# Attention scores in four half-height products, row sums in PSUM and head loads on one queue

## The chip, the cores and the metric

The kernel runs on one core of a Trainium2 chip. The engines that matter here are TensorE (PE in the profile), VectorE (DVE), ScalarE (ACT), GpSimd (POOL, which here only starts DMA transfers and clears a few tiles) and SyncE (SP, which only starts DMA transfers). Matmul results go to PSUM, which has eight banks of 512 fp32 values per partition. The metric is the device time of one execution in microseconds. Of the kernel before, three runs gave a median of 1306.28 us (1305.25 to 1308.36).

## The reference

Attention over 8 batches, 8 heads, 576 tokens and a head size of 64, in which every score more than tau below its row's maximum is dropped, is followed by a two-layer network on 4608 rows of 512 with a rational activation:

```python
scores = scale * np.matmul(q, k.transpose(0, 1, 3, 2))
thresh = np.max(scores, axis=-1, keepdims=True) - tau
scores = np.where(scores >= thresh, scores, -1000000000.0)
scores = scores - np.max(scores, axis=-1, keepdims=True)
attn = np.exp(scores)
attn = attn / (np.sum(attn, axis=-1, keepdims=True) + 1e-09)
x = np.matmul(attn, v)            # then heads side by side: 4608 x 512
h = x @ w_in                      # 512 x 2048
P = a[0] + a[1] * h + a[2] * h2 + a[3] * h3          # h2 = h*h, h3 = h2*h
Q = 1.0 + np.abs(b[0]) * np.abs(h) + np.abs(b[1]) * h2
out = (P / (Q + 1e-06)) @ w_out   # 2048 x 512
```

## The kernel before

**Units.** Attention is worked in units. A full unit is 128 query rows of a pair of heads of one batch (32 pairs, four full units each, 128 in all); a rest unit holds the last 64 query rows of both heads (32 in all). The pairs are visited twice or once each, in a fixed order of 160 units. A pair's queries lie in one tile QQ, head 0 on partitions 0 to 63 and head 1 on 64 to 127, its keys likewise in KK; there are two buffers of each.

**One full unit** goes through these steps.

- Scores (f_qk, lines 805 and 809). Two fp32 products over 64 partitions, one per head, give the first 512 keys; a third over 128 partitions, from key columns that are zero in the other head's half, gives the last 64 keys of both heads. The scores fill three banks of PSUM. The first 21 units alternate between banks 0 to 2 and banks 3 to 5; from then on every unit uses banks 0, 1 and 2, so a unit's products can start only when the unit before has been read. Head 0 has columns 0 to 575 of the three banks, head 1 columns 960 to 1535, so the middle bank, bank 1, holds the tail of head 0 and the head of head 1.
- Row maximum (line 815, DVE), threshold (822 on ACT or 824 on DVE).
- Per head a Prelu activation on ACT (830) that moves the scores from PSUM into an SBUF tile e. When both heads are through, the three banks are free.
- Per head an exponential on ACT (834), in place in e, whose row sum is written by a second record, ACTIVATION_READ_ACCUMULATOR, into a small SBUF tile st.
- The sum's reciprocal (839 on ACT or 841 on DVE, then 845 on DVE), the probabilities as a high and a low fp16 part (339 or 341, and 856), two DMA transposes from SP (866), and the product with the values (925).

**The network** is worked in chunks: first-layer products (1042), a move to SBUF on ACT (1051), a chain of about ten elementwise steps that alternates between DVE and ACT (1056 to 1092), and second-layer products (1101).

**What sets the order.** The program is straight-line code. A planner (class Plan) is given each operation with an engine, a duration, a key and the operations that it needs, and lists them by a simple timetable of its own; two tables, TURN and KIND, shift the keys. Every engine then executes its own list strictly in that order, and an instruction that waits holds up everything behind it on its engine. The planner knows the buffers and the banks of the scores, and reckons with the times at which they come free. The waits in the built program come from the layer below, which follows what each instruction reads and writes and adds semaphores; two engines that touch the same PSUM bank are put in program order by it. The planner has "DMA" for SP and "GD" for POOL among its engines. Loads of queries and keys of the first eight pairs go out from SP, later ones from POOL; the two visits' first key loads from ACT.

Of the kernel before, what the change touches and what calls it, by code (L numbers as in the profile page):

```python
# [16 lines left out]
AX = mybir.AxisListType  # L17

# [19 lines left out]
SINGLE = 21  # L38
# [12 lines left out]

FROM_ACT = 2
# [25 lines left out]
EARLY = {"ACT": 1.2900, "DVE": 3.3863}  # L78
EARLY_END = 714.5248
PRICE = {"ACT": 1.0645, "DVE": 2.1978}  # L80

TURN = [
# [21 lines left out]
KIND = [  # L104
# [8 lines left out]
LOADS_END = 120.0  # L113
# [22 lines left out]
class Plan:  # L136
# [20 lines left out]
    def op(self, eng, dur, key, fn, after=(), take=(), drop=()):  # L157
        engs = {eng: dur} if isinstance(eng, str) else eng
        o = Op(engs, key, fn, [x for x in after if x is not None], list(take), list(drop))
        o.turn, o.kind = self.turn, self.kinds.setdefault(fn.__code__, len(self.kinds))  # L160
# [26 lines left out]
    def order(self):  # L187
# [19 lines left out]
        left = len(self.ops)  # L207
        while left:
# [38 lines left out]
            if e == "DMA" and o.drop and t < LOADS_END:  # L247

                o.dur = 2.0 * o.dur + 1.0
# [22 lines left out]
            for d in o.then:  # L272
                d.wait -= 1
                for x in d.engs:
                    d.ready[x] = max(d.ready[x], end + (self.OWN[e] if x == e else self.TO.get((e, x), self.LAT[e])))
# [14 lines left out]
def masked_attention_rational_ffn(  # L290
# [86 lines left out]
    QW = S + REM  # L377
    QQs = [const.tile([P, QW], F32, name=f"QQ{i}") for i in range(NQ)]
    KKs = [const.tile([P, QW + REM], F32, name=f"KK{i}") for i in range(NQ)]
    for t in QQs:  # L380
        nc.gpsimd.memset(t[:, NT * P:], 0.0)
    for t in KKs:
        nc.gpsimd.memset(t[0:D, S:QW], 0.0)
        nc.gpsimd.memset(t[D:P, 0:REM], 0.0)
# [899 lines left out]
```

## Time and profile before

| | |
|---|---|
| median of three runs | 1306.28 us |
| the profiled execution, its own time | 1312.41 us |
| its span | 1310.6 us |
| TensorE clock granted | 0.986 |
| busy: PE, DVE, ACT, POOL | 1253.8, 1217.9, 1114.4, 243.4 us |

The profile is of one execution. Busy time of PE is from modelled ends of pipelined matmuls, so that one matmul overlaps the next; busy times of DVE and ACT are those of their instructions. A name such as "banks" is the PSUM tile, "L834" is a line of the kernel before. In the kernel after, the same lines stand some lines lower: the scores at 807, the exponential at 840, the reciprocal's first step at 845 and 847, the transposes at 872, the two layers at 1048 and 1107.

### The profile page before, as it was taken

The numbers are of one execution on the slowest core, as the hardware profiler recorded it, in microseconds if no ns is written. First come the engines' busy times: TensorE is split into PE (matmuls) and PEld (weight loads), VectorE is DVE, ScalarE is ACT, GpSimd is POOL, SyncE is SP. The second block draws the span as 40 slices with busy tenths as digits, with TensorE's granted clock in tenths as the row PEclk, the third lists the DMA queues.
The fourth block names the chain that finished last, engine by engine and source line by source line (L and its number), as shares of the span: only waits on it lengthen the run. The fifth ranks groups of instructions, "written<-read, shape, count | busy, mean of one in ns | idle before, by whom it ended". The sixth has DMA issues, their size and how long they took to land. (4 is left out here: it accounts for less than half of the span.)

```text
span 1310.6 us, 25351 instructions
## 1 busy us (share of the span) xinstructions
PE 1253.8 (96%) x9430; PEld 931.8 (71%) x9430; DVE 1217.9 (93%) x1913; ACT 1114.4 (85%) x2182; POOL 243.4 (19%) x462
## 2 busy tenths in 40 slices
PE   8898989999999999998999979999999999999998
PEld 6576677777677777776777657766677777778886
DVE  5899999999999999988999979999999999999777
ACT  5898998999999999997999878978998798885564
POOL 1101100023213220323112231223213221110000
PEclk8998999999999999999999989999999999999999
DMA  7433454476656565677554875676756654563000
GB/s 206 132 116 125 142 128 87 105 160 119 124 116 134 124 131 107 117 143 129 95 103 96 115 132 100 122 126 119 137 106 115 132 131 75 109 111 55 17 17 17
DMA packets 340587, 146.66 MB, mean 112 GB/s; under 512 B 316208, under 2 KB 323184, under 8 KB 340464
## 3 DMA queue, kind: packets, MB, share of 16 engines
q1 hardware_dynamic: 316400, 86.49, 37.4%
q0 software_dynamic: 22784, 57.31, 16.4%
q8 instruction: 74, 1.21, 0.4%
q10 hardware_dynamic: 1280, 1.25, 0.4%
q14 instruction: 49, 0.40, 0.1%
HBM read 60.30 MB, written 9.44 MB: 53 GB/s over the span
## 5 line engine op out<-in xcount | busy, mean ns | idle before, releaser
L1101 PE MATMUL banks<-wp,g 128*128 128x512 f32 x1728 | 442.1, 404 | 1.6 <-DVE g L1092 1.2
L1042 PEld LDWEIGHTS <-wi 128*128 128x128 f16 x3456 | 333.6, 98 | 67.1 <-issue 29.0
L1042 PE MATMUL banks<-x,wi 128*128 128x256 f16 x3072 | 360.8, 274 | 10.0 <-ACT t L1051 9.3
L1101 PEld LDWEIGHTS banks<-wp,g 128*128 128x128 f32 x1728 | 315.9, 189 | 75.3 <-DVE g L1092 4.0
L834 ACT ACTIVATE e<-e,cf 128x576 f32<-128x576 f32 x288 | 222.1, 778 | 0.2
L856 DVE SCALAR_TENSOR_TENSOR e<-e,st,hi 128x576 f16<-128x576 f32 x252 | 204.6, 812 | 7.5 <-ACT hi L339 6.4
L339 ACT ACTIVATE hi<-e,st 128x576 f16<-128x576 f32 x223 | 169.6, 769 | 46.8 <-DVE st L845 30.8
L830 ACT ACTIVATE e<-banks,st 128x576 f32<-128x576 f32 x288 | 206.3, 737 | 3.0 <-DMA pT<-e 0.8
L815 DVE TENSOR_REDUCE st<-banks 128x2 f32<-128x1152 f32 x128 | 172.4, 1347 | 16.2 <-PE banks L809 15.8
L805 PE MATMUL banks<-KK,QQ 64*128 64x512 f32 x512 | 154.0, 650 | 7.2 <-DVE t L346 3.9
L925 PE MATMUL banks<-pT,V 128*64 128x256 f16 (+1 forms) x2520 | 122.8, 250 | 12.8 <-DMA pT<-e 10.2
L1051 ACT ACTIVATE t<-banks,hsc 128x512 f32<-128x512 f32 (+1 forms) x192 | 106.1, 574 | 30.3 <-PE banks L1042 24.5
L925 PEld LDWEIGHTS <-V 128*64 128x64 f16 x2520 | 105.0, 111 | 34.0 <-issue 22.7
L809 PEld LDWEIGHTS banks<-KK,QQ 128*128 128x128 f32 x256 | 38.6, 190 | 99.1 <-issue 94.6
L1078 DVE SCALAR_TENSOR_TENSOR t<-t,co,t 128x1024 f32<-128x1024 f32 (+1 forms) x73 | 92.3, 1265 | 17.4 <-ACT t L1072 17.1
L1069 ACT ACTIVATE t<-t,co 128x1024 f32<-128x1024 f32 (+1 forms) x73 | 82.8, 1134 | 29.6 <-DVE t L1065 24.1
L1092 DVE TENSOR_TENSOR g<-t,g 128x512 fp32r<-128x512 f32 x144 | 95.0, 684 | 3.1 <-ACT g L331 2.9
L650 POOL DMA_DIRECT2D QQ<-in_qT_dram x42 | 22.2, 529 | 381.0 <-PE banks L809 194.8
L1084 DVE SCALAR_TENSOR_TENSOR t<-t,co,t 128x1024 f32<-128x1024 f32 (+1 forms) x73 | 92.3, 1265 | 0.6
L1075 DVE SCALAR_TENSOR_TENSOR t<-t,co,t 128x1024 f32<-128x1024 f32 (+1 forms) x73 | 92.2, 1264 | 0.1
L1065 DVE SCALAR_TENSOR_TENSOR t<-t,co 128x1024 f32<-128x1024 f32 (+1 forms) x73 | 92.3, 1264 | 0.0
L1062 DVE SCALAR_TENSOR_TENSOR t<-t,co 128x1024 f32<-128x1024 f32 (+1 forms) x73 | 92.2, 1263 | 0.0
(128 smaller groups left out, 1545.3 us busy)
## 6 DMA issues: line engine op xcount, KB each, us to landing
t<-in_w_in_dram POOLq DMA_DIRECT2D x16, 512.0 KB, 5.3
t<-in_w_out_dram POOLq DMA_DIRECT2D x16, 512.0 KB, 4.1
out_dram<-u POOLq DMA_DIRECT2D x26, 256.0 KB, 2.9
V<-in_v_dram POOLq DMA_DIRECT2D x24, 256.0 KB, 4.5
QQ<-in_qT_dram POOLq DMA_DIRECT2D x42, 144.0 KB, 2.8
KK<-in_kT_dram POOLq DMA_DIRECT2D x42, 144.0 KB, 3.2
QQ<-in_qT_dram POOLq DMA_DIRECT2D x42, 128.0 KB, 2.9
KK<-in_kT_dram POOLq DMA_DIRECT2D x42, 128.0 KB, 2.8
```

Source lines behind the costliest of these rows:

```text
L339: nc.scalar.activation(dst, src, AF.Identity, scale=factor)
L805: nc.tensor.matmul(d, QQ[r, t * P:(t + 1) * P], KK[r, REM:S], **one)
L815: nc.vector.tensor_reduce(box["st"][:, 0:2], box["both"], AX.X, ALU.max, negate=True)
L830: nc.scalar.activation(ev(hh), box["s"][hh], AF.Prelu, scale=SCALE, bias=box["st"][:, 2 + hh:3 + hh], alpha=STEEP)
L834: nc.scalar.activation(e, e, AF.Exp, scale=passes, accum_out=box["st"][:, 4 + hh:5 + hh])
L856: nc.vector.scalar_tensor_tensor(box["lo"][:, c], ev(hh), box["st"][:, 6 + hh:7 + hh], box["hi"][:, c], ALU.mult, ALU.subtract)
L925: nc.tensor.matmul(dst, V[:, c * P + hh * D:c * P + (hh + 1) * D], rhs, start=c == 0 and n == 0, stop=c == NT and n == 2)
L1042: nc.tensor.matmul(d, wi_tile(c, f0 + j, hl), x[:, c, :], start=c == 0 and n == 0, stop=c == NC - 1 and n == 2)
L1051: nc.scalar.activation(box["h3"][:, 2 * k:2 * k + 2, sl], psv[:, :, sl], AF.Identity, scale=hsc[:, b2, g:g + 1])
L1065: nc.vector.scalar_tensor_tensor(box["q"], box["q"], bc, box["q"], ALU.add, ALU.mult)
L1092: nc.vector.tensor_tensor(fr(g[:, 1]), box["r"][:, k * GW:(k + 1) * GW], g[:, 0], ALU.subtract)
L1101: nc.tensor.matmul(acc[tt], fr(g[:, x]), fr(wo[f][y]), start=begins and j == n == 0, stop=ends and j == nb - 1 and n == 2)
```

## The change

- **Scores.** f_qk of a full unit issues four products over 64 partitions: head 0's last 64 keys (into bank 1), head 1's first 512, head 0's first 512, and head 1's last 64 (into bank 1). The third product over 128 partitions is gone, and with it the zeroed columns of KK. Before the fourth product an instruction without work waits for the first one, as both write bank 1.
- **Sums.** From unit 21 on the exponential writes its row sum not into st but into PSUM, in a part of bank 1 that no score uses (columns 64 to 79 of the bank, two per unit, eight units in turn). The reciprocal's first step reads it there.
- **Loads.** A head's keys come in one transfer of 64 by 576 where there were up to three per half; the queries' last piece is loaded only in visits with a rest unit. All loads of queries and keys go out from SP, save the first two keys, which stay with ACT.
- **Planner.** Transfers have a time on a common "wire" that adds up. Tables and weights are other numbers, and the order of the work on every engine changes with them.

Shortened to its core:

```diff
+EARLY_QK = 32
...
-    -1608, -5790, -5238, -4368, -3938, -1990, -1002, -997, -1155, -1814, -1674, -918, -35, -495, -954, -211, -329,
+    1227, 1843, 340, -6090, -1991, -677, -1314, -1454, -1244, -1773, -184, 498, -1335, 117, -424, 727, 1242, 421,
...
+            if o.wire is not None:
+                wire = max(wire, t + BEGIN) + o.wire[0]
+                seen = max(wire, end + 1.0) + o.wire[1]
...
-        queue, eng = (nc.sync, "DMA") if bp < EARLY_BP else (nc.gpsimd, "GD")
+        act = bp < FROM_ACT and ts[0] == 0
+        queue, eng = (nc.sync, "DMA") if bp < EARLY_QK else (nc.gpsimd, "GD")
...
-            kq_.dma_start(KK[0:D, REM:S], kT[bb, pr, :, 0:NT * P])
-            kq_.dma_start(KK[D:P, REM:QW], kT[bb, pr, :, S + REM:])
-            kq_.dma_start(KK[0:D, 0:REM], kT[bb, pr, :, NT * P:S])
-            if NT in ts:
-                for i in range(2):
-                    kq_.dma_start(KK[i * D:(i + 1) * D, QW:], kT[bb, pr, :, NT * P + i * REM:S + i * REM])
+            for hh, c in (0, 0), (1, S + REM):
+                kq_.dma_start(KKs[kh.slot][hh * D:(hh + 1) * D, :], kT[bb, pr, :, c:c + S])
...
-            for hh in range(2):
+            for hh, k0, n, d0 in (0, NT * P, REM, NT * P), (1, 0, NT * P, w - NT * P), (0, 0, NT * P, 0), (1, NT * P, REM, w - S):
                 r = slice(hh * D, (hh + 1) * D)
-                d = s[:, 0:NT * P] if hh == 0 else s[:, w - NT * P:]
-                nc.tensor.matmul(d, QQ[r, t * P:(t + 1) * P], KK[r, REM:S], **one)
-            dst, src = (bass.AP(x.tensor, x.offset, [list(x.ap[0]), [n, 2], [1, REM]])
-                        for x, n in ((s[:, NT * P:S], w - 2 * NT * P - REM), (KK[:, 0:REM], S)))
-            nc.tensor.matmul(dst, QQ[:, t * P:(t + 1) * P], src, **one)
+                if d0 == w - S:
+                    tc.add_manual_dep(nc.tensor.nop().ins, shared.ins.name, ORDERED, reason="one bank")
+                mm = nc.tensor.matmul(s[:, d0:d0 + n], QQ[r, t * P:(t + 1) * P], KK[r, k0:k0 + n], **one)
+                if d0 == NT * P:
+                    shared = mm
...
+        def total(h0, h1):
+            if single:
+                return box["st"][:, 4 + h0:4 + h1]
+            o = S - 512 + 2 * (place_of[bp, t] % 8)
+            return ps[:, 1, o + h0:o + h1]
...
-            nc.scalar.activation(e, e, AF.Exp, scale=passes, accum_out=box["st"][:, 4 + hh:5 + hh])
+            nc.scalar.activation(e, e, AF.Exp, scale=passes, accum_out=total(hh, hh + 1))
```

**Where instructions moved.** Three places of the program are shown, each before and after. In the brackets stand the semaphores that a row waits for: PE_49, DVE_49 and Activation_49 count what these engines have finished, DMAHW and DMASW count landed transfers.

The first place is ACT at unit 64 (counted from 0, a full unit, buffers e_78 and st_84), from its Prelus to the sum's step. Before:

```order
L830 ACTIVATE e_78<-banks,st_84 128x576 [waits DMAHW3_49,Activation_49]
L1051 ACTIVATE t_73<-banks,hsc 128x512 [waits PE_49]
L830 ACTIVATE e_78<-banks,st_84 128x576
L834 ACTIVATE e_78,st_84<-e_78,cf 128x576 [waits Activation_49]
L935 ACTIVATE x_98<-banks 128x256 [waits PE_49]
L834 ACTIVATE e_78,st_84<-e_78,cf 128x576 [waits Activation_49]
L1056 ACTIVATE t_69<-t_73 128x1024 [waits DVE_49]
```

After:

```order
L830 ACTIVATE e_78<-banks,st_84 128x576 [waits DMAHW5_49,Activation_49]
L830 ACTIVATE e_78<-banks,st_84 128x576
L840 ACTIVATE e_78,banks<-e_78,cf 128x576 [waits Activation_49]
L840 ACTIVATE e_78,banks<-e_78,cf 128x576 [waits PE_49,Activation_49]
L1057 ACTIVATE t_72<-banks,hsc 128x512
L845 ACTIVATE st_84<-banks 128x2 [waits Activation_49]
L1062 ACTIVATE t_73<-t_72 128x1024 [waits Activation_49]
```

The exponentials write "banks" where they wrote st, and the second of them waits for PE as well: by the semaphore's count, for the last score product of unit 65. The step on the sum reads "banks".

The second place is PE at the scores of unit 65, the next unit. Before:

```order
L925 MATMUL banks<-pT_83,V_164 64x256
L805 MATMUL banks<-KK_114,QQ_112 128x512 [waits DVE_49,Activation_49]
L805 MATMUL banks<-KK_114,QQ_112 128x512 [waits Activation_49]
L809 MATMUL banks<-KK_114,QQ_112 128x2x64
L1101 MATMUL banks<-wp_0_155,g_96 128x512 [waits DVE_49] x2
```

After:

```order
L1048 MATMUL banks<-x_97,wi 128x256
L807 MATMUL banks<-KK_116,QQ_112 128x64 [waits DVE_49,Activation_49]
L807 MATMUL banks<-KK_116,QQ_112 128x512 x2
L807 MATMUL banks<-KK_116,QQ_112 128x64 [waits PE_49]
L1107 MATMUL banks<-wp_0_147,g_95 128x512
```

Before, the wait for ACT is for the two Prelus of unit 64. After, by the count, the first product waits for the first exponential of unit 64, and the fourth, through the instruction without work, for the first product. Over the whole program 64 full units' scores wait for the first exponential of the unit before and 24 for the second; 59 second and 14 first exponentials wait for the scores of the next unit, 52 of the 59 standing right behind the first; and 43 of the sum's steps on ACT wait for such scores.

The third place is SP in the middle of the program. Before:

```order
L866 DMA_TRANSPOSE pT_83<-hi_80 128x9x128 [waits DMAHW5_49,PE_49,Activation_49]
L866 DMA_TRANSPOSE pT_83<-e_78 128x9x128 [waits DMAHW7_49,DVE_49]
L866 DMA_TRANSPOSE pT_83<-hi_80 128x9x128 [waits DMAHW3_49,Activation_49]
L866 DMA_TRANSPOSE pT_83<-e_79 128x9x128 [waits DMAHW4_49,DVE_49]
L866 DMA_TRANSPOSE pT_82<-hi_80 128x5x128 [waits DVE_49,PE_49,Activation_49]
```

After:

```order
L872 DMA_TRANSPOSE pT_83<-hi_80 128x9x128 [waits DMAHW7_49,PE_49,Activation_49]
L652 DMA QQ_112<-in_qT_dram 64x576 [waits DMAHW0_49,PE_49]
L653 DMA QQ_112<-in_qT_dram 64x512 [waits DMAHW1_49]
L872 DMA_TRANSPOSE pT_83<-e_77 128x9x128 [waits DMAHW2_49,DVE_49]
L660 DMA KK_116<-in_kT_dram 64x576 [waits DMAHW3_49]
L660 DMA KK_116<-in_kT_dram 64x576 [waits DMAHW4_49]
L872 DMA_TRANSPOSE pT_83<-hi_81 128x9x128 [waits DMAHW5_49,Activation_49]
```

Loads of queries and keys stand between the transposes, and the first of each waits for PE to have finished with the buffer.

More of the change, by code (lines that the diff above doesn't have):

```diff
@@ L76 @@
         "gh": {"ACT": 0.52, "DVE": 0.33}, "wh": {"ACT": 0.57, "DVE": 0.38}}
-EARLY = {"ACT": 1.2900, "DVE": 3.3863}
+EARLY = {"ACT": 1.4729, "DVE": 3.6245}
 EARLY_END = 714.5248
-PRICE = {"ACT": 1.0645, "DVE": 2.1978}
+PRICE = {"ACT": 0.7602, "DVE": 2.1876}
 TURN = [
[21 rows of a table removed]
[21 rows of a table added]
 KIND = [
[4 rows of a table removed]
[4 rows of a table added]
 TOL = {"PE": 0, "ACT": 0.129, "DVE": 0.1, "POOL": 0.1, "DMA": 0, "GD": 0}
 WARM, WARM_END = 0.6, 400.0
-LOADS_END = 120.0
+BEGIN = 1.4
 class Op:
@@ L155, in pool, with op @@
         self.pools[name] = [(0.0, i) for i in range(n)]
-    def op(self, eng, dur, key, fn, after=(), take=(), drop=()):
+    def op(self, eng, dur, key, fn, after=(), take=(), drop=(), wire=None):
         engs = {eng: dur} if isinstance(eng, str) else eng
         o = Op(engs, key, fn, [x for x in after if x is not None], list(take), list(drop))
+        o.wire = wire
         o.turn, o.kind = self.turn, self.kinds.setdefault(fn.__code__, len(self.kinds))
@@ L274, in order @@
                 for x in d.engs:
-                    d.ready[x] = max(d.ready[x], end + (self.OWN[e] if x == e else self.TO.get((e, x), self.LAT[e])))
+                    d.ready[x] = max(d.ready[x], seen if o.wire is not None else
+                                     end + (self.OWN[e] if x == e else self.TO.get((e, x), self.LAT[e])))
                     if not d.wait:
@@ L374, in masked_attention_rational_ffn @@
     ones = bass.AP(one.tensor, one.offset, [list(one.ap[0]), [0, P]])
-    QW = S + REM
-    QQs = [const.tile([P, QW], F32, name=f"QQ{i}") for i in range(NQ)]
-    KKs = [const.tile([P, QW + REM], F32, name=f"KK{i}") for i in range(NQ)]
+    QQs = [const.tile([P, S + REM], F32, name=f"QQ{i}") for i in range(NQ)]
     for t in QQs:
         nc.gpsimd.memset(t[:, NT * P:], 0.0)
-    for t in KKs:
-        nc.gpsimd.memset(t[0:D, S:QW], 0.0)
-        nc.gpsimd.memset(t[D:P, 0:REM], 0.0)
+    KKs = [const.tile([P, S], F32, name=f"KK{i}") for i in range(NQ)]
     nc.vector.tensor_scalar(passes, cf[:, 6:7], 0.0, None, ALU.is_ge)
@@ L489, in ld @@
             if not loaded:
-                for x in KKs[0][:, REM:REM + 1], QQs[0][:, 0:1]:
+                for x in KKs[0][:, 0:1], QQs[0][:, 0:1]:
                     nc.gpsimd.tensor_scalar(cf[:, 15:16], x, 1.0, 1.0, ALU.mult, ALU.mult)
@@ L523, in f6 @@
                 tensor_tensor(dst.bitcast(I32), t, box["rw"][:, :, 0], ALU.add)
-        l = op("GD", 2.5, key - 2.0, ld, (), [hold])
+        l = op("GD", 2.5, key - 2.0, ld, (), [hold], wire=(1.75, 2.0))
         if i < NC:
@@ L651, in ldq @@
             queue.dma_start(QQ[D:P, 0:NT * P], qT[bb, pr, :, S + REM:])
-            queue.dma_start(QQ[D:P, S:], qT[bb, pr, :, S:S + REM])
+            if NT in ts:
+                queue.dma_start(QQ[D:P, S:], qT[bb, pr, :, S:S + REM])
         def ldk():
-            KK = KKs[kh.slot]
-            kq_ = nc.scalar if bp < FROM_ACT else queue
-            kq_.dma_start(KK[0:D, REM:S], kT[bb, pr, :, 0:NT * P])
-            kq_.dma_start(KK[D:P, REM:QW], kT[bb, pr, :, S + REM:])
-            kq_.dma_start(KK[0:D, 0:REM], kT[bb, pr, :, NT * P:S])
-            if NT in ts:
-                for i in range(2):
-                    kq_.dma_start(KK[i * D:(i + 1) * D, QW:], kT[bb, pr, :, NT * P + i * REM:S + i * REM])
-        q_done[bp] = [op(eng, 4.3 if first else 1.6, p0, ldq, (), [qh])]
-        k_done[bp] = [op(eng, 0.1 if bp < FROM_ACT else 1.6, p0 + 0.1, ldk, (), [kh])]
+            kq_ = nc.scalar if act else queue
+            for hh, c in (0, 0), (1, S + REM):
+                kq_.dma_start(KKs[kh.slot][hh * D:(hh + 1) * D, :], kT[bb, pr, :, c:c + S])
+        issue = {"DMA": 1.25, "GD": 1.1}[eng]
+        q_done[bp] = [op(eng, 3.1 if first else issue + (0.6 if NT in ts else 0.0), p0, ldq, (), [qh], wire=(0.75, 1.0))]
+        k_done[bp] = [op(eng, 0.1 if act else issue, p0 + 0.1, ldk, (), [kh], wire=(0.75, 1.0))]
+    place_of = {u: i for i, u in enumerate(units)}
     def is_plain(bp, t):
@@ L705, in load_v_ops @@
         q = bp * (NT + 0.5) - 17.0
-        l = v_loaded[bp] = op(eng, 1.6, max(q, V0 + V1 * pr), ld, (), [vhold])
+        l = v_loaded[bp] = op(eng, 1.7, max(q, V0 + V1 * pr), ld, (), [vhold], wire=(0.95, 1.5 if eng == "DMA" else 2.5))
         hv = [Hold("u", 1)]
@@ L766, in unit_ops @@
         full = t < NT
-        single = units.index((bp, t)) < SINGLE
+        single = place_of[bp, t] < SINGLE
         heads = (0, 1) if full else (0,)
@@ L794, in f_qk @@
                 s = box["s"][0] = s[:, 0:S]
-                for k0, c0, n in (REM, 0, NT * P), (QW, NT * P, REM):
-                    nc.tensor.matmul(s[:, c0:c0 + n], QQ[:, NT * P:QW], KK[:, k0:k0 + n], **one)
+                for c0, n in (0, NT * P), (NT * P, REM):
+                    nc.tensor.matmul(s[:, c0:c0 + n], QQ[:, NT * P:], KK[:, c0:c0 + n], **one)
                 return
@@ L947, in unit_ops @@
         need = k_done[bp] + q_done[bp]
-        qk = op("PE", 1.47 if full else 1.12, p, f_qk, need, [sh[0]], [kh, qh] * nh)
+        qk = op("PE", 1.36 if full else 1.12, p, f_qk, need, [sh[0]], [kh, qh] * nh)
         if full:
@@ L957, in unit_ops @@
         for hh in heads:
-            mk[hh] = op("ACT", 0.76, p + 0.3 + 0.02 * hh, lambda hh=hh: f_sum(hh), [ex[hh]])
+            mk[hh] = op("ACT", 0.735, p + 0.3 + 0.02 * hh, lambda hh=hh: f_sum(hh), [ex[hh]])
         rec = op(FLEX["rec"], 0, p + 0.4, f_rec, list(mk.values()))
@@ L982, in unit_ops @@
             tp = op("DMA", TPD if full else 0.6 * TPD, p + 0.6, lambda: f_tp("hi"), his + two["tp"], [two["pT"]] if t % 2 == 0 else (),
-                    [hi_hold])
-            tp = op("DMA", TPD if full else 0.6 * TPD, p + 0.65, lambda: f_tp("lo"), los + [tp], (), [e_hold])
+                    [hi_hold], wire=(1.2 if full else 0.65, 0.8))
+            tp = op("DMA", TPD if full else 0.6 * TPD, p + 0.65, lambda: f_tp("lo"), los + [tp], (), [e_hold], wire=(1.2 if full else 0.65, 0.8))
             two["tp"].append(tp)
@@ L1187, in moe_ops @@
                 if through:
-                    op("DMA" if late else "GD", 0.6 if kind == "m" else 1.1, p + 2.3, lambda tt=tt: f_st(tt), [o], (), [ho])
+                    op("DMA" if late else "GD", 0.6 if kind == "m" else 1.1, p + 2.3, lambda tt=tt: f_st(tt), [o], (), [ho], wire=(0.75, 1.0))
                 else:
```

9 lines of the change are left out of this document (4 added, 5 removed), and 48 rows, old and new, of tables (KIND, TURN).

## The prediction

> **What bounds the kernel now.** I read the page's busy shares first, then the chain of work that ended last, then the windows by stage, and last the table of waits.
>
> ```profile
> PE 1253.8 (96%) x9430; PEld 931.8 (71%) x9430; DVE 1217.9 (93%) x1913; ACT 1114.4 (85%) x2182; POOL 243.4 (19%) x462
> DVE 19%; ACT 4%; issue 4%; PE 2%; DMA 1%; ACTq 0%; DVEq 0%
> ```
>
> No engine alone sets the time: PE and DVE are both above 90%, and the chain passes among them. The stages tell more (PE, PEld, DVE, ACT and POOL in this order):
>
> ```profile
> 0.00:180.00 180.00, 160.15 (x1101) 116.24 (x1102) 154.56 (x356) 153.00 (x341) 22.52 (x58) 0.95 0.49 143
> 180.00:1170.00 990.00, 958.17 (x7383) 705.18 (x7382) 949.09 (x1424) 878.26 (x1705) 219.78 (x402) 0.99 0.61 118
> 1170.00:1311.00 141.00, 135.49 (x960) 110.39 (x954) 114.25 (x135) 83.17 (x137) 1.12 (x2) 1.00 0.14 29
> ```
>
> In the middle stage, which holds the units from 21 on, PE is idle for 990.00 - 958.17 = 32 us, DVE for 41 and ACT for 112. So PE and DVE set the pace there, and ACT has a reserve of 11%. That reserve is what this change draws on. The waits show how little of it is spent on any one cause:
>
> ```profile
> POOL QQ L650 <- PE banks L809: 194.8, 20, 25.7
> ACT hi L339 <- DVE st L845: 30.8, 40, 1.5
> ACT t L1051 <- PE banks L1042: 24.5, 15, 4.1
> DVE t L1078 <- ACT t L1072: 17.1, 9, 2.4
> PEld banks L805 <- ACT e L830: 10.5, 17, 4.1
> PE banks L925 <- DMA pT<-e: 10.2, 9, 5.2
> ```
>
> POOL's long wait is a parked load of queries and costs nothing. PE waits 10.5 us in all for the Prelus that free the score banks, and DVE 17.1 us for ACT within the network.
>
> **The sums in bank 1.** This is the part that decides. Before, the exponential writes its sum to SBUF and has nothing to do with the score banks. After, it writes bank 1, into which the next unit's first and fourth product go, and the built program puts the two engines in order. Unit 64 of before, ACT and then PE, shows what now overlaps:
>
> ```profile
> 484.21 0.74 ACT L830 ACTIVATE e<-banks,st 128x576 f32<-128x576 f32 x1
> 484.84 0.78 ACT L834 ACTIVATE e<-e,cf 128x576 f32<-128x576 f32 x1
> 485.50 0.21 ACT L834 ACTIVATION_READ_ACCUMULATOR e<-e,cf 128x1 f32 x1
> 485.81 0.38 ACT L935 ACTIVATE x<-banks 128x256 f16<-128x256 f32 x1
> 486.09 0.77 ACT L834 ACTIVATE e<-e,cf 128x576 f32<-128x576 f32 x1
> 486.76 0.19 ACT L834 ACTIVATION_READ_ACCUMULATOR e<-e,cf 128x1 f32 x1
> 485.70 1.13 PE L805 MATMUL banks<-KK,QQ 64*128 64x512 f32 x4
> 486.76 0.49 PE L809 MATMUL banks<-KK,QQ 128*128 128x128 f32 x2
> 487.00 1.18 PE L1101 MATMUL banks<-wp,g 128*128 128x512 f32 x4
> ```
>
> The banks are free at 484.21 + 0.74 = 484.95. The first sum is written by 485.50 + 0.21 = 485.71, and the next unit's scores run from 485.70 to 486.76 + 0.49 = 487.25. The second exponential starts at 486.09, in the midst of them. In the new order the scores must wait for the first sum (up to 485.71 - 484.95 = 0.76 us of PE time, nothing here), and the second exponential for the end of the scores: ACT would stand from 485.71 to 487.25, 1.5 us, with everything behind it on ACT.
>
> The counts are those of the order above; the prices are 1.5 us less what stands between on ACT.
>
> - 52 second exponentials right behind the first: 52 x 1.5 = 78 us.
> - 7 with a copy of L935 (0.38) between: 7 x 1.1 = 8 us.
> - 14 first exponentials that wait for the next scores. Mostly a part of the probabilities (the L339 row below, 0.77) stands between: 14 x 0.7 = 10 us.
> - 43 sum steps on ACT that wait for the next scores: 13 right behind an exponential, 1.5 each; 13 behind a copy, 1.1; 17 behind other work, 0.6 taken: 20 + 14 + 10 = 44 us.
>
> ```profile
> L339 ACT ACTIVATE hi<-e,st 128x576 f16<-128x576 f32 x223 | 169.6, 769 | 46.8 <-DVE st L845 30.8
> L834 ACT ACTIVATION_READ_ACCUMULATOR e<-e,cf 128x1 f32 x288 | 58.1, 202 | 0.0
> ```
>
> That makes 140 us in which ACT can do nothing. Bounds: below, 78 + 8 = 86 us if only the second exponentials count; above, about 200 if PE reaches the scores late and ACT waits for the work ahead of them too. On PE, 64 scores wait up to 0.76 us for a first sum and 24 for a second one, up to 486.76 + 0.19 - 484.95 = 2.0 us; I take 0.25 and 0.5, nearer to nothing because the scores often start later than the banks come free: 16 + 12 = 28 us, between 0 and 97. The Trainium skill speaks for the wait itself: "PSUM — Partial Sum Buffer", section "PSUM bank collisions raise a hardware error", has two engines kept apart by bank and quadrant, not by address. If addresses alone counted, no wait would be needed and this part of the sum would be nothing; the order shows that the program goes by the bank, and no run here shows a collision.
>
> The readout of the sum goes to PSUM instead of SBUF. The next ACT instruction starts about 0.1 us after it starts, so at most 0.1 x 288 = 29 us is to be won; the trace has no such write to PSUM. I take 5 us, near nothing, with 0 and 29 as ends.
>
> **The scores.** Today they take from L805's start to L1101's, 487.00 - 485.70 = 1.30 us. The nearest row for 512 and 64 columns one after the other is a rest unit, on 128 rows:
>
> ```profile
> 399.77 1.19 PE L796 MATMUL banks<-KK,QQ 128*128 128x512 f32 x4
> 400.80 0.27 PE L1042 MATMUL banks<-x,wi 128*128 128x256 f16 x1
> ```
>
> It takes 1.03 us. If both halves run side by side, the four products cost that and a change of tile height before them and after them. So one end is a gain of 0.27 us. If the two short products overlap with nothing, they take 2 x 1.03 x 64/576 = 0.23 us in place of the 0.24 us of L809 (486.76 to 487.00): no gain. The other end, both halves in turn, is 2 x 1.03 - 1.30, a loss of 0.76 us. That the halves do run side by side is seen in L805: four passes in 1.13 us. The change of height was within the scores and now comes behind them. I take a gain of 0.06 us, 8 us over 128 units (ends: -35 and +97). The wait ahead of the fourth product is for one that ended long before; it costs nothing unless the halves don't overlap. The Trainium skill, "TensorE: Matmul & The Clock Gate", Part 3, section "The mechanism", says that matmuls start and end strictly in program order. By that rule head 1 would start with head 0's last pass and L805 would be three passes long, some 1.3 us by L796's pace, which the 1.13 us contradict; the new scores would then lose some 0.2 us each, an estimate of 26 us in all.
>
> **The loads.** POOL gives up 42 visits of six or more transfers. SP gets them in fewer pieces:
>
> ```profile
> L650 SPq DMA_DIRECT2D QQ<-in_qT_dram x14: 465/466/594, 1.5 to 264.0; - x14
> L866 SPq DMA_TRANSPOSE pT<-hi x140: 1200/1292/2063, 177.3 to 1189.2; - x140
> KK<-in_kT_dram POOLq DMA_DIRECT2D x42, 144.0 KB, 3.2
> ```
>
> SP then issues 252 loads of queries and keys at 0.47 us, 118 us (84 loads, 39 us, before), beside 280 transposes at 1.3 us, 364 us: it has room. What is new is that a load that waits for PE holds the transposes behind it, and PE waits for these (10.2 us above). A load stands where the planner expects its buffer, so it is late by as much as the scores are late, 0.3 us or so: some 40 loads x 0.3 = 12 us, hidden by the two pT buffers; I take 0, ends -5 and +30. The planner's new tables can win no more than PE's 32 us of idle time in the middle stage; nothing in the trace tells whether they do. I take 0.
>
> **The sum**, for the middle stage. ACT needs 878 + 140 - 5 = 1013 us of 990: 23 us longer if ACT never waits for anything else. A tenth of its 112 us is taken to stay, 11 us. PE needs 958 + 28 - 8 = 978, which fits. So +34 us: a span of 1345, and 1312.41 + 34 = 1346 for the profiled execution. That execution is 6 us above the median of the runs, and I make the forecast from the median: 1306 + 34 = **1340 us**, 2.6% slower. Own range of this case: +10 (the sum steps' waits cost little) to +79 (half of ACT's old idle time stays), 1316 to 1385.
>
> **The rivals.**
>
> - *Faster: PE and DVE still set the end.* If ACT's waits of today vanish because it is late anyway, and the sum steps don't bind, 878 + 86 - 5 = 959 us fits into 990. From ACT's forced waits below about 112 us on, this decides. PE then gains half of the 0.27 us per scores, 17 us, and the planner a few of the 32 us: -20 us, 1286. For it: ACT is 89% busy in the stage and DVE waits for it in few places. Against it: the waits fall right at the exponentials, on which probabilities and DVE hang.
> - *No change.* Both in balance, 1306; the same row speaks for it.
> - *The four products don't run as pairs*, the strict order above: some +26 us on PE besides the waits, 1365.
> - *SP's queue becomes a wait of PE for transposes*, +30 us on top, 1370. For it: a transpose took up to 2063 ns to issue; against it: PE waits only 10.2 us for them.
>
> **How the numbers follow.** ACT's waits decide: 0.50. Strict order 0.05, SP's queue 0.07: both slower. No change 0.09. Faster 0.29. Slower is then 0.62. The likeliest case gives 1340. To hold 8 in 10 the range must reach into the faster case, to its -20: 1286; and at the top to 1382, just below the upper end of the likeliest case. A difference of 0.2%, 2.6 us, is about what a measurement of this kernel can tell from none.
>
> **What would show it.** In the profile after, second exponentials (L840) should show idle time before them put down to PE's L807, some 1.5 us each and 60 to 90 us in all, and the sum steps (L845) some more. ACT's idle time in the middle stage should be no smaller than 112 us, and DVE should wait for ACT at hi, at the reciprocal and at the step that was L1078 by tens of us. The four products should take 1.2 to 1.3 us. If L840 shows no such waits, or ACT's idle time only changes its names and PE stays above 96% of the stage, the forecast is wrong.

## The result, and the profile after

The kernel after takes 1406.87 us (median of four runs, 1406.33 to 1412.31), the kernel before in the same session 1305.76 us: a ratio of 1.0781 [1.0749, 1.0812], 101 us slower. The direction was forecast, the size was not: 1340 us, with 1382 as the upper end.

The page of the kernel after, busy shares and the chain that ended last:

```profile
PE 1261.3 (90%) x9700; PEld 973.7 (69%) x9700; DVE 1224.1 (87%) x1910; ACT 1125.5 (80%) x2187; POOL 83.8 (6%) x158
ACT 8%; DVE 8%; PE 7%; issue 2%; DMA 1%; SPq 0%; ACTq 0%; DVEq 0%
```

The work on PE, DVE and ACT is within 1% of what it was; every share is lower, because the span grew from 1310.6 to 1404.8 us, 94 us. (The medians differ by 101 us, as the profiled execution of the kernel before was 6 us above its median.) The stage that was 180 to 1170 us now ends 90 us later (window, length, then PE, PEld, DVE, ACT and POOL as in the prediction):

```profile
180.00:1260.00 1080.00, 960.60 (x7601) 733.96 (x7599) 949.61 (x1424) 880.19 (x1691) 60.45 (x102) 0.98 0.53 106
```

PE's busy time is 960.60 (958.17 before), DVE's 949.61 (949.09), ACT's 880.19 (878.26). So all 90 us are idle time, and not of one engine: PE stands 119 us (32 before), DVE 130 (41), ACT 200 (112). Each of the three gained about 88 us. With the same work in a longer stage it can't be otherwise; what it says is that no engine has more to do than before, and that the time went into waiting. The table of waits names the pairs:

```profile
PEld banks L807 <- ACT e L840: 106.2, 80, 6.7
ACT e L840 <- PE banks L807: 90.6, 60, 2.7
PE banks L807 <- ACT e L840: 73.5, 70, 3.3
DVE st L851 <- ACT st L845: 48.4, 56, 2.9
ACT st L845 <- PE banks L807: 40.2, 32, 3.0
DVE st L847 <- ACT e L840: 32.9, 24, 3.3
DVE st L815 <- ACT st L845: 18.0, 15, 1.8
PE banks L797 <- ACT e L840: 6.9, 10, 1.2
```

(Engine, tile and line, whom it waited for; us in all, times, the longest. PEld is the weight load that stands ahead of a matmul, so its row and PE's overlap and are not added.) None of these rows had a counterpart of this size before. Unit by unit it looks like this; here is the unit whose exponentials start at 510.38 us, ACT, PE and DVE, with what each waited for in brackets:

```profile
510.38 0.78 ACT L840 ACTIVATE e<-e,cf 128x576 f32<-128x576 f32 x1
...
511.06 0.15 ACT L840 ACTIVATION_READ_ACCUMULATOR e<-e,cf 128x1 f32 x1
511.26 1.35 PE L807 MATMUL banks<-KK,QQ 64*128 64x64 f32 x8 [0.64 <-ACT e L840]
...
512.54 3.06 PE L1107 MATMUL banks<-wp,g 128*128 128x512 f32 x12
512.75 0.78 ACT L840 ACTIVATE e<-e,cf 128x576 f32<-128x576 f32 x1 [1.54 <-PE banks L807]
...
514.05 0.17 ACT L845 ACTIVATE st<-banks 128x2 f32<-128x2 f32 x1
...
514.26 0.17 DVE L851 RECIPROCAL st<-st 128x2 f32<-128x2 f32 x1 [1.38 <-ACT st L845]
```

PE stands 0.64 us until the first exponential has left its sum; then it makes the next unit's scores, and ACT stands 1.54 us until they are done; then the second exponential runs, the sum's step follows, and DVE stands 1.38 us until it has the sum. On this path each step begins only when the step of another engine has ended; what the engines have beside it (DVE is in the network while ACT stands) runs out at different times, and then they stand too.

### The profile page after: what moved, and what is told of

The parts are those of the page before. It is cut to its first block, busy times and chain, and to the rows that moved or that the text cites. A ratio compares the mean times of both kernels' runs of the same rounds, so it can differ in the third digit from the quotient of the medians.

```text
span 1404.8 us, 25929 instructions
## 1 busy us (share of the span) xinstructions
PE 1261.3 (90%) x9700; PEld 973.7 (69%) x9700; DVE 1224.1 (87%) x1910; ACT 1125.5 (80%) x2187; POOL 83.8 (6%) x158
## 5 line engine op out<-in xcount | busy, mean ns | idle before, releaser
L1107 PE MATMUL banks<-wp,g 128*128 128x512 f32 x1728 | 448.0, 406 | 13.0 <-DVE g L1098 7.1
L1048 PE MATMUL banks<-x,wi 128*128 128x256 f16 x3072 | 364.5, 275 | 11.3 <-ACT t L1057 8.6
L840 ACT ACTIVATE e<-e,cf 128x576 f32<-128x576 f32 x288 | 223.6, 777 | 102.8 <-PE banks L807 90.6
L807 PE MATMUL banks<-KK,QQ 64*128 64x512 f32 (+1 forms) x1024 | 178.2, 460 | 87.6 <-ACT e L840 73.5
L807 PEld LDWEIGHTS banks<-KK,QQ 64*128 64x128 f32 x1024 | 117.3, 190 | 163.6 <-ACT e L840 106.2
L344 ACT ACTIVATE hi<-e,st 128x576 f16<-128x576 f32 x220 | 167.5, 769 | 17.4 <-DVE st L851 14.6
L1057 ACT ACTIVATE t<-banks,hsc 128x512 f32<-128x512 f32 (+1 forms) x192 | 106.3, 578 | 21.3 <-PE banks L1048 14.6
L1084 DVE SCALAR_TENSOR_TENSOR t<-t,co,t 128x1024 f32<-128x1024 f32 (+1 forms) x73 | 92.2, 1263 | 16.9 <-ACT t L1078 16.6
L1087 DVE SCALAR_TENSOR_TENSOR t<-t,t 128x1024 f32<-128x1024 f32 (+1 forms) x73 | 87.9, 1204 | 0.7
```

The source lines that it names most:

```text
L344: nc.scalar.activation(dst, src, AF.Identity, scale=factor)
L807: mm = nc.tensor.matmul(s[:, d0:d0 + n], QQ[r, t * P:(t + 1) * P], KK[r, k0:k0 + n], **one)
L840: nc.scalar.activation(e, e, AF.Exp, scale=passes, accum_out=total(hh, hh + 1))
L1048: nc.tensor.matmul(d, wi_tile(c, f0 + j, hl), x[:, c, :], start=c == 0 and n == 0, stop=c == NC - 1 and n == 2)
L1057: nc.scalar.activation(box["h3"][:, 2 * k:2 * k + 2, sl], psv[:, :, sl], AF.Identity, scale=hsc[:, b2, g:g + 1])
L1107: nc.tensor.matmul(acc[tt], fr(g[:, x]), fr(wo[f][y]), start=begins and j == n == 0, stop=ends and j == nb - 1 and n == 2)
```

## The experiments

All kernels have the unit order, tables and loads of the kernel named. "Sums in st" means that the row sums go to SBUF as before the change; where waits are then put back "by hand", an instruction is made to wait for the last exponential, sum step or score product issued ahead of it on the other engine, with nothing else changed. For full units these are the waits that PE and ACT have for each other in the kernel after. For rest units they are stronger: there the waiting stands ahead of the first product, while in the kernel after only the second one, which writes bank 1, has to wait. Times are medians; ratios are to the kernel before of the same session.

### Is it the sums?

**The change without the sums** (`st_sums`):

```diff
         def total(h0, h1):
-            if single:
+            if True:
                 return box["st"][:, 4 + h0:4 + h1]
```

> The kernel after with the row sums back in SBUF (st); products, loads and order of the work as after. Theory A (sharing bank 1 makes the loss, by the waits between the scores and the exponentials): about 1300 us, 1285 to 1315, so 95 to 120 us under the kernel after, and no waits between L807 and L840 beyond those for the Prelus. Rival B (the new order of the work, the four products or the loads on SP carry a good part of it): 1330 to 1390 us.

1293.0 us, ratio 0.9901 [0.9864, 0.9937]: not only is the whole loss gone, the rest of the change makes the kernel 1% faster. Its page:

```profile
PE 1238.8 (96%) x9700; PEld 969.6 (75%) x9700; DVE 1215.5 (94%) x1910; ACT 1116.5 (86%) x2187; POOL 85.5 (7%) x158
```

So with this order of the work the sums in bank 1 cost 114 us.

**The sums alone** (`before_bank1`), put into the kernel before:

```diff
+        def total(h0, h1):
+            if single:
+                return box["st"][:, 4 + h0:4 + h1]
+            o = S - 512 + 2 * (units.index((bp, t)) % 8)
+            return ps[:, 1, o + h0:o + h1]
...
-            nc.scalar.activation(e, e, AF.Exp, scale=passes, accum_out=box["st"][:, 4 + hh:5 + hh])
+            nc.scalar.activation(e, e, AF.Exp, scale=passes, accum_out=total(hh, hh + 1))
```

> The kernel before with one part of the change alone: row sums from unit 21 on in bank 1, read from there by the reciprocal's first step. Three products, loads and order as before. Theory A: about 1400 us, 1380 to 1420, the whole loss of the change. Rival B: 1320 to 1360 us, a part of it only. By the recorded sum (34 us from ACT's and PE's waits) 1340 us.

1358.64 us, 1.0417 [1.0388, 1.0446]: 53 us, neither the whole loss nor the forecast. Here only the third, short product writes bank 1, at the end of the scores. The same sums are worth 53 us in one kernel and 114 us in the other, and the number of waits does not tell why: 79 exponentials and 37 sum steps wait for scores here, 73 and 43 after.

### Which waits?

Next the waits were put back into `st_sums`, one direction at a time. ACT's (`act_waits`):

```diff
-            nc.scalar.activation(e, e, AF.Exp, scale=passes, accum_out=total(hh, hh + 1))
+            i = nc.scalar.activation(e, e, AF.Exp, scale=passes, accum_out=total(hh, hh + 1)); single or tc.add_manual_dep(i.ins, prior["Q"], ORDERED, reason="order")
```

and the same on the sum's step on ACT, where prior["Q"] is the last score product issued so far.

> The kernel after with the row sums in st, but with the waits that ACT has in the kernel after put back by hand: 73 exponentials and 43 sum steps wait for the scores that stand ahead of them in the program (the same counts as after). PE waits for the Prelus only. The recorded sum's view (ACT's forced waits decide, PE's hardly cost): close to the kernel after, 1380 to 1410 us. Theory A1 (the two directions together make a loop exponential - scores - exponential, and each alone is partly hidden): 1320 to 1360 us.

PE's (`pe_waits`), with prior["E"] the last exponential issued so far:

```diff
-            box["s"][0], box["s"][1] = s[:, 0:S], s[:, w - S:]
+            box["s"][0], box["s"][1] = s[:, 0:S], s[:, w - S:]; "E" in prior and tc.add_manual_dep(nc.tensor.nop().ins, prior["E"], ORDERED, reason="order")
```

> The kernel after with the row sums in st, but with PE's waits put back by hand: each unit's scores from unit 21 on wait for the last exponential that stands ahead of them in the program, 130 waits against 119 in the kernel after. ACT waits for no scores. The recorded sum (28 us of PE, of which part is hidden): 1300 to 1325 us. Theory A1 (PE's waits cost as much as ACT's): 1335 to 1370 us.

Both edits together (`both_waits`):

> The kernel after with the row sums in st, with the waits of both directions between PE and ACT put back by hand (scores for the last exponential, exponentials and sum steps for the last scores). Alone they cost 41 us (ACT's) and 24 us (PE's) over 1293. If the two only add: 1350 to 1362 us. Theory A1 (a loop: a late exponential delays the scores, which delay the next exponential): 1375 to 1410 us.

ACT's alone 1333.81 us (1.0221 [1.0189, 1.0252]), 41 us over `st_sums`; PE's alone 1317.2 us (1.01 [1.007, 1.013]), 24 us; both 1402.16 us (1.0741 [1.0707, 1.0775]), 109 us. The two together cost 44 us more than the one and the other. The tables of waits show it in the waits themselves. With ACT's alone:

```profile
ACT e L840 <- PE banks L807: 60.0, 60, 2.2
ACT st L845 <- PE banks L807: 12.1, 17, 2.0
```

with PE's alone:

```profile
PE banks L807 <- ACT e L840: 31.9, 47, 4.8
```

with both:

```profile
ACT e L840 <- PE banks L807: 90.7, 60, 2.7
PE banks L807 <- ACT e L840: 74.0, 73, 6.3
DVE st L851 <- ACT st L845: 61.3, 67, 3.1
ACT st L845 <- PE banks L807: 41.0, 32, 2.6
```

The same 60 waits of the exponential last 1.0 us each in the one kernel and 1.5 us in the other: PE comes later with the scores, because it has itself waited for the exponential. And PE's waits double, because ACT comes later with the exponential. (Part of the 109 us belongs to the stronger waits of the rest units: the three rows between L797 and ACT are 17.0, 14.6 and 14.2 us here, 6.9, 4.7 and 7.0 in the kernel after. So it is not a measure of how much of the 114 us PE and ACT make between them.)

**DVE's waits** (`all_waits`). The row maximum (815) reads bank 1 too. In the kernel after it is in order with the exponentials and sum steps that stand ahead of it, and they with it. These waits were added to `both_waits`, and with them the waits between scores and sum steps on DVE (847):

> As both_waits, and also the waits that DVE's row maximum has with ACT in the kernel after (row maximum for the last exponential or sum step, and these for the row maximum ahead of them), DVE's own sum steps too: the same kinds and nearly the same counts of waits as after, only the sums lie in SBUF. Theory W (the waits are the whole loss): within 10 us of the kernel after, 1397 to 1417 us. Rival P (writing and reading the sums in PSUM itself costs, by slower records or by disturbing PE): 1355 to 1375 us, the rest being the access itself.

1421.03 us, 1.0882 [1.0853, 1.091]: another 19 us, a little above the 1397 to 1417 expected. The row of DVE in the profile is the one of the kernel after to the digit, although the sums are in SBUF; the rows of the rest units are larger (6.9, 4.7 and 7.0 us in the kernel after):

```profile
DVE st L815 <- ACT st L845: 18.0, 15, 1.8
PE banks L797 <- ACT e L840: 19.7, 16, 2.0
ACT st L845 <- PE banks L797: 15.1, 11, 2.3
ACT e L840 <- PE banks L797: 13.5, 10, 1.7
L840 ACT ACTIVATION_READ_ACCUMULATOR e<-e,cf 128x1 f32 x288 | 56.5, 196 | 0.0
```

The kernel after, with the sums really in PSUM, is 14 us *faster* than this (1406.87, in another session whose kernel before differs by 0.8 us). So the waits suffice for the whole loss without the sums in PSUM. How the 14 us divide is not shown. The rest units wait 30 us less in the kernel after, and of such waits 40 to 67% ended up in the time in the runs tabled below: an estimate of 12 to 20 us, enough for all of it. The record that writes the sum is also shorter in PSUM, by 10 us of ACT's time in all:

```profile
L840 ACT ACTIVATION_READ_ACCUMULATOR e<-e,cf 128x1 f32 x288 | 46.3, 161 | 0.0
```

### Is it a loop?

The waits can be pictured as a loop: exponential, next scores, next exponential. If so, its length decides and not the number of waits. A first attempt changed the order of the four products in the kernel after. Both that write bank 1 ahead (`bank1_first`), so that the exponential waits for less:

```diff
-            for hh, k0, n, d0 in (0, NT * P, REM, NT * P), (1, 0, NT * P, w - NT * P), (0, 0, NT * P, 0), (1, NT * P, REM, w - S):
+            for hh, k0, n, d0 in (0, NT * P, REM, NT * P), (1, NT * P, REM, w - S), (1, 0, NT * P, w - NT * P), (0, 0, NT * P, 0):
```

> The kernel after with the four products in another order: both that write bank 1 first (the 64-column ones), then the two of 512. The waits between PE and ACT are as many as after, but an exponential waits for two short products only, not for all of the scores. Theory A1 (the loop exponential - scores - exponential sets the time, so what shortens it pays): 1340 to 1385 us; the second short product's wait for the first, some 0.2 us on PE in 107 units, costs 20 us of the gain at most. Rival (the count of the waits decides, not what lies inside them): 1400 to 1425 us.

or both at the end (`bank1_last`), so that PE works beside the exponential:

```diff
-            for hh, k0, n, d0 in (0, NT * P, REM, NT * P), (1, 0, NT * P, w - NT * P), (0, 0, NT * P, 0), (1, NT * P, REM, w - S):
+            for hh, k0, n, d0 in (1, 0, NT * P, w - NT * P), (0, 0, NT * P, 0), (0, NT * P, REM, NT * P), (1, NT * P, REM, w - S):
```

> The kernel after with the two products of 512 columns first and both that write bank 1 last, so that PE works beside the exponential and waits only ahead of the short products; as many waits as after. Theory A1: 1335 to 1375 us. Rival (the count of the waits decides): 1400 to 1425 us.

1404.05 us (1.0738 [1.0711, 1.0765]) and 1395.91 us (1.0679 [1.0656, 1.0701]): against my expectation almost nothing. But these two did not test what they should. The scores themselves became slower, by the row of `bank1_first` (it was 178.2 us in the kernel after):

```profile
L807 PE MATMUL banks<-KK,QQ 64*128 64x64 f32 (+1 forms) x1024 | 233.7, 476 | 69.0 <-ACT e L840 51.6 <-DMA KK<-in_kT_dram 3.7 <-ACT e L830 3.3
```

That is 55 us, 0.43 us a unit, where I had allowed 20. In the order of the change a short product of one head stands next to a long one of the other, and they run side by side; two short ones in a row that wait for each other lose that: in one unit of `bank1_first` (at 581.17 us) the second short product starts 0.58 us after the first, while in the kernel after the long one that stands next starts 0.01 us after it. ACT's waits for L807 did fall (from 131 to 92 us in `bank1_first`), but PE paid for it. Inconclusive.

The second attempt leaves the products alone and moves only the waits of `both_waits`. In `late_wait` PE waits ahead of the fourth product instead of the first; in `early_free` ACT waits for the first product instead of the fourth:

```diff
-            box["s"][0], box["s"][1] = s[:, 0:S], s[:, w - S:]; "E" in prior and tc.add_manual_dep(nc.tensor.nop().ins, prior["E"], ORDERED, reason="order")
+            box["s"][0], box["s"][1] = s[:, 0:S], s[:, w - S:]
...
                 if d0 == w - S:
+                    "E" in prior and tc.add_manual_dep(nc.tensor.nop().ins, prior["E"], ORDERED, reason="order")
```

> As both_waits (sums in st, waits of both directions between PE and ACT by hand, 1402 us), but PE's wait for the exponential stands ahead of the fourth product only, so that three products run beside the exponential; the order of the products, and so their own time, is as after. Loop theory A1 (the length of exponential - scores - exponential decides): 1345 to 1378 us, since up to 0.76 us of each second exponential's wait goes. Rival (the number of handshakes decides, not what lies inside them): 1390 to 1405 us.

```diff
-                mm = nc.tensor.matmul(s[:, d0:d0 + n], QQ[r, t * P:(t + 1) * P], KK[r, k0:k0 + n], **one); prior["Q"] = mm.ins.name
+                mm = nc.tensor.matmul(s[:, d0:d0 + n], QQ[r, t * P:(t + 1) * P], KK[r, k0:k0 + n], **one)
                 if d0 == NT * P:
-                    shared = mm
+                    shared = mm; prior["Q"] = mm.ins.name
```

> As both_waits, but the exponentials and the sum steps wait for the first of the four products only instead of the fourth; as many waits, products in the same order. Loop theory A1: 1320 to 1360 us, since about 1.0 us of each of ACT's waits goes and PE's stay. Rival (the number of handshakes decides): 1390 to 1405 us.

1354.87 us (1.0383 [1.0358, 1.0408]) and 1342.44 us (1.0285 [1.0254, 1.0315]). With as many waits, 47 and 60 of the 109 us are gone. The unit shown above, in `early_free`:

```profile
488.45 0.78 ACT L840 ACTIVATE e<-e,cf 128x576 f32<-128x576 f32 x1
489.11 0.20 ACT L840 ACTIVATION_READ_ACCUMULATOR e<-e,cf 128x1 f32 x1
489.68 1.35 PE L807 MATMUL banks<-KK,QQ 64*128 64x64 f32 x8
490.15 0.78 ACT L840 ACTIVATE e<-e,cf 128x576 f32<-128x576 f32 x1 [0.83 <-PE banks L807]
```

The second exponential starts in the midst of the scores; it stands 0.83 us instead of 1.54. So it is the length of the loop that decides, from both of its ends.

**The sum's steps** (`no_rec`): `both_waits` without the 43 waits of L845.

> As both_waits, without the 43 waits of the sum steps for the scores. In the recorded sum these steps are 44 of ACT's 140 us. If they take their share of the 109 us: 1360 to 1378 us. If scores and exponentials alone make the loop: 1388 to 1403 us.

1386.5 us, 1.0621 [1.0596, 1.0646], between the two ranges. These steps hold 16 of the 109 us. In the table below (rows of PE for L840 and of ACT for the products of L807 and L797, summed) scores and exponentials alone still make PE and ACT stand 187 us:

| kernel | ACT waits for scores, us | PE waits for exponentials, us | over `st_sums`, us |
|---|---|---|---|
| `act_waits` | 81 | 0 | 41 |
| `pe_waits` | 0 | 36 | 24 |
| `early_free` | 72 | 51 | 49 |
| `late_wait` | 108 | 20 | 62 |
| `no_rec` | 108 | 78 | 94 |
| `both_waits` | 161 | 91 | 109 |

In each of them between 40 and 67% of the two columns ends up in the time; the rest is taken out of idle time that the engines had anyway. (PE's waits for the Prelus are not in the table; they are 16.3 us in `st_sums`, 24.0 in `act_waits`, 22.2 in `late_wait`.) The forecast let a fifth of them through (34 of 140 + 28 us).

### Is it the order, the products, or the loads?

**The products.** The four products alone in the kernel before (`before_four`): the part "Scores" of the change's diff, with the key tiles and the one transfer per head's keys that go with them, on the queues of before.

> The kernel before with the four products alone, with the key tiles without zeroed columns and one transfer per head's keys that belong to them; loads on the queues of before, order as before. The recorded sum: 8 us less, 1298 us, between 1271 (the halves run side by side throughout) and 1403 us (in turn). By the strict-order rival some 26 us more, 1332 us.

1299.89 us, 0.9955 [0.9935, 0.9974]: 6.6 us less. The other way round, that same part taken out of the kernel after, with the sums in bank 1 (`after_three`) and in st (`st_three`):

> The kernel after with the three products of before (the third, over 128 partitions, alone writes bank 1, at the end) and their key tiles and transfers, sums in bank 1, order as after. Theory A1 (the sums cost 53 us with these products in the order of before because only the last, short product waits): 1340 to 1362 us. Rival (the new order of the work made the sums cost 114 us instead of 53): 1395 to 1420 us.

> As after_three (three products of before in the order of after, 1371 us), with the row sums in st. If the products are worth the same in both orders (6.6 us): 1295 to 1306 us, and then the sums cost 65 to 76 us with these products, against 114 us with the four. If the four products are worth more in the new order: 1310 to 1330 us.

1371.32 us (1.0488 [1.0464, 1.0513]) and 1310.48 us (1.0035 [1.0012, 1.0057]). So with three products the sums cost 61 us in the new order of the work and 53 us in the old one: the order makes 8 us of difference. With four products they cost 114 us in the same order. The difference of 53 us lies in the products: the first of the four already writes bank 1 and so waits for the exponential, with the other three behind it. That fits `late_wait`, where moving this wait alone behind the first three products was worth 47 us: the length of the loop once more. (The four products are worth 17 us here, with their one transfer per head's keys, against 6.6 in the order of before.)

**The loads.** `st_sums` with the loads of queries and keys sent from POOL again, at the same places of the order (`st_pool_loads`):

```diff
-        queue, eng = (nc.sync, "DMA") if bp < EARLY_QK else (nc.gpsimd, "GD")
+        queue, eng = (nc.sync if bp < EARLY_BP else nc.gpsimd, "DMA") if bp < EARLY_QK else (nc.gpsimd, "GD")
```

> The kernel after with the row sums in st and the loads of queries and keys from the ninth pair on sent from POOL instead of SP, at the same places of the order. The recorded sum (SP's loads cost nothing): 1290 to 1296 us, as with the sums in st alone (1293). Rival (loads on SP hold transposes back): 1270 to 1288 us. Rival (POOL delivers later): over 1297 us.

1307.27 us, 1.0012 [0.999, 1.0034]: 14 us slower than from SP. In the table of waits the values' loads, which POOL sends too, now come late (2.1 us in `st_sums`):

```profile
POOL QQ L652 <- PE banks L797: 275.6, 18, 36.9
ACT u L704 <- DMA V<-in_v_dram: 10.1, 4, 4.4
```

POOL is parked on a load of queries, and the values stand behind it. That this is the whole of the 14 us is argued, not shown.

**A planner that knows** (`aware`): the planner is told that a unit's banks come free only with the step that reads its sum.

```diff
-                        [thr[hh]] + ([ex[0]] if hh else []), [e_hold] if hh == 0 else (), [sh[hh]])
+                        [thr[hh]] + ([ex[0]] if hh else []), [e_hold] if hh == 0 else (), [sh[hh]] if single else ())
...
-        rec = op(FLEX["rec"], 0, p + 0.4, f_rec, list(mk.values()))
+        rec = op(FLEX["rec"], 0, p + 0.4, f_rec, list(mk.values()), (), () if single else list(sh.values()))
```

> The kernel after, sums in bank 1, but the planner is told that a unit's score banks come free only after the step that reads its sum; it places the next scores behind that step (101 scores wait for it, no exponential and no sum step waits for scores). The order of the work changes on every engine. If the order can hide the wait (scores to sum is some 6 us of a unit's 8): 1295 to 1330 us. If not (banks held longer leave PE idle): 1330 to 1400 us.

1412.45 us, 1.0814 [1.0777, 1.0851]. The waits of exponentials for scores are gone, but the scores come so late that ACT waits for the row maximum instead (22.7 us in the kernel after):

```profile
ACT st L822 <- DVE st L815: 86.0, 61, 8.2
```

By these rows the way from one unit's scores to the next one's is longer, not shorter. Whether tables made for this rule would do better was not tried.

## Why the prediction was wrong

**What bounds the kernel, and where the change bites: right.** It named the sums in bank 1 as the part that decides, and the order between exponential and scores as its mechanism. `st_sums` shows that without the sums there is no loss; how much they cost hangs on the products (61 us with three, 114 with four).

**ACT's forced waits, 140 us: right.** The rows above and those of the rest units give 90.6 + 7.0 for the exponentials and 40.2 + 4.7 for the sum's steps, 142.5 us, and 90.6 us in 60 waits is 1.51 us each, against 1.5.

```profile
L840 ACT ACTIVATE e<-e,cf 128x576 f32<-128x576 f32 x288 | 223.6, 777 | 102.8 <-PE banks L807 90.6 <-PE banks L797 7.0
L845 ACT ACTIVATE st<-banks 128x2 f32<-128x2 f32 (+1 forms) x106 | 18.0, 170 | 51.2 <-PE banks L807 40.2 <-DVE st L815 5.9 <-PE banks L797 4.7
```

**The sum: here it failed.** The step was "A tenth of its 112 us is taken to stay, 11 us. PE needs 958 + 28 - 8 = 978, which fits." It treated ACT and PE as two accounts, paid each engine's waits out of its own idle time, and took the longer. Measured in the middle stage: ACT 880 busy + 142.5 waiting for scores leaves 57 us of its 1080 for other idle time, not 11. So half of the old idle time stayed, not a tenth, and that term alone is 46 of the 56 us by which the stage outran the forecast (90 against 34). The tenth had no row behind it, and ACT's old waits show why it was too little: that for the row maximum stayed whole, those for the first-layer products (24.5 us before) and at hi (30.8) fell to 14.6 us each. Before, for the row maximum, and then the three rows after:

```profile
ACT st L822 <- DVE st L815: 23.2, 19, 9.4
...
ACT st L822 <- DVE st L815: 22.7, 20, 8.9
ACT t L1057 <- PE banks L1048: 14.6, 12, 2.8
ACT hi L344 <- DVE st L851: 14.6, 31, 1.5
```

The case "half of ACT's old idle time stays" stood in the prediction as the upper end of its own range, +79; the stage came out at +90.

`act_waits` shows that the step fails already without PE's waits. ACT's waits are 81 us there, which by the sum fit into the reserve of 112 us (98 in `st_sums`, 180 to 1150 us) and cost nothing; they cost 41 us. (That 41 is near the forecast's 34 is chance.)

The second account was mis-sized too. On PE the waits for exponentials were not 28 us but 73.5 + 6.9 = 80 us, within the bounds (0 to 97) but near their top; with them the sum itself would have had PE at 958 + 80 - 8 = 1030 of 990. And the accounts are not separate: with PE's waits put in, ACT's grow from 81 to 161 us, PE's from 36 to 91, and the time by 44 us more than the two alone. The 1.5 us per exponential already contained PE's own wait (the scores that start only after the first sum), so the sum had the loop in its price and left it out of its balance. (The lower end of that range, +10, does not come out of the sum either: without the sum steps' 44 us ACT would need 969 us, which fits.)

**DVE: a missed term.** The text counted the order between ACT and PE only. The row maximum reads the same bank, and DVE's sum steps too; the waits of DVE put in together cost 19 us.

**The readout, -5 us (0 to -29): sign right for the record, its worth not shown.** It took 161 ns instead of 199 with the sums in st, 11 us of ACT's time in 288 records; what of that reached the time is not separated (the 14 us between `all_waits` and the kernel after hold the rest units' waits too). The Trainium skill, "ScalarE: Activation LUTs", "Step-by-step: what each stage is for", says that ScalarE reaches PSUM faster than SBUF; the 161 against 199 ns agree.

**The four products, -8 us: right,** 6.6 measured, and 512.54 - 511.26 = 1.28 us a unit where 1.2 to 1.3 was said. The rival of a strict order of the products, +26 us, falls with it: `before_four` has the other sign. (The rule of the Trainium skill behind it, "TensorE: Matmul & The Clock Gate", Part 3, "The mechanism", that matmuls start and end strictly in program order, does not describe these passes if the program has them in the order of the calls: in the unit that the prediction shows, head 1's first pass starts 0.007 us after head 0's first and 0.53 us ahead of head 0's second. In which order the built program has the passes is not on record.)

**The loads, 0 (-5 to +30): outside its bounds, on the good side,** -14 us against POOL in the order made for SP. (The order itself, with POOL's loads, is 7 us slower than `before_four`, so loads and order together come to some -6.) The rival that SP's queue would hold back the transposes falls: in the kernel after SP stands 128.6 us at loads of queries until the scores have left a buffer free, and PE waits 3.5 us for the transposes of e, against 10.2.

```profile
SPq L652 <- PE banks L807: 128.6, 25, 25.1
PE banks L931 <- DMA pT<-e: 3.5, 4, 1.4
```

**The rival "faster"** gave a point from which it decides: ACT's forced waits below about 112 us. They were 142.5. But `act_waits`, with 81, was slower than `st_sums` by 41 us as well. So the rival's ground (that PE and DVE go on setting the pace while ACT spends its reserve) is wrong, not only its number.

**The signs.** L840's idle time before L807, 90.6 us, came at the upper edge of the 60 to 90 named; L845 followed; ACT's idle time was above 112. DVE waited at the reciprocal, as said, but not at hi nor at L1084 (16.6 us, 17.1 before).

The whole change, from the runs: four products -6.6, loads and order of the work another -6, ACT's waits alone +41, PE's alone +24, the two as a loop +44, DVE's waits +19, and -14 from `all_waits` to the kernel after (sums in PSUM and shorter waits of the rest units, not separated): 1306 to 1407. Each term is a difference of two neighbouring runs, so that they add up is no proof of any one of them.

## What to carry to other kernels

A wait that engine A has for B and one that B has for A, on the same buffer, are not two costs to be paid out of two reserves: try each alone and both together, and look whether the waits themselves get longer. Before something small is put into a free corner of a PSUM bank, list every engine that touches the bank, reads too, and ask which of them now stands in order with which; if it must be, let the first instruction behind the wait be as late, and the one that releases it as early, as can be. A reserve of idle time seen in a profile is not all there to be drawn on, as part of it is waiting for other engines that are late as well; of this kernel's 112 us on ACT half was no use.

## What was not expected of the hardware

Two short products that write one bank, one right behind the other and waiting for it, cost 0.43 us more per unit than the same four with the halves alternating (233.7 against 178.2 us over 128 units, and 231.7 us with the two at the end): in the unit looked at, the second began only 0.58 us after the first. And the record that writes the activation's sum was shorter into PSUM than into SBUF, 161 against 199 ns; what that is worth in the kernel's time no run here separates.
